# Linear attention and routed experts: the transposed q in two banks of its own, a tail step earlier, another front order

## The chip, the cores and the metric

The kernel runs on one core of a Trainium2 chip. Its engines work side by side, each through a queue of its own in order: PE multiplies matrices into PSUM, DVE and ACT do elementwise work and read PSUM, POOL does elementwise work in SBUF and issues loads, SP issues most other DMAs. The metric is the time of the program on the device in microseconds (us). The kernel before takes 950.27 us, the median of 3 runs from 950.16 to 950.39.

## What is computed

Inputs are q, k, v of shape (8, 8, 576, 64): 8 batches, 8 heads, 576 positions, 64 channels. Linear attention comes first, then a layer of 8 experts over 4608 tokens of 512 channels, weighted by a routing matrix that is normalised eight times over rows and columns.

```
phi(x) = where(x > 0, x, exp(x) - 1) + 1
q_p, k_p = phi(q), phi(k)
kv = einsum('bhsd,bhse->bhde', k_p, v);  z = sum(k_p, axis=2)
x  = (q_p @ kv) / (q_p . z + 1e-06)          # regrouped to (4608, 512)
P  = exp(x @ w_gate - max)
8 times: P /= P.sum(1) + 1e-09; P /= P.sum(0) + 1e-09; P *= 4608 / 8
out = sum over e of P[:, e] * (relu(x @ w1[e]) @ w2[e])
```

w1 is (8, 512, 1024), w2 is (8, 1024, 512).

## The kernel before

The program has three parts: a front, in which the attention is computed and expert 0 fills the gaps; a long middle, in which experts 1 to 7 run; and a tail for the last group of tokens.

**Attention by half batches.** The function att(b, g) handles four heads of a batch, half batch n = 2b + g, n from 0 to 15. Loads of k, q and v come through POOL's queue (n = 0 partly through SP's). Each kind has three buffers, so a load waits until the work on the load three before it is done. From k, ACT makes Exp and DVE makes max(x + 1, 1) and then the minimum of both, which is phi(k). PE multiplies it with v (f_kv, 64 x 64 tiles of the array). For q, PE transposes first (f_qt), into PSUM; ACT takes Exp of the transposed q (f_qe, L537), DVE the max (f_qm, L541), and DVE the minimum of both in SBUF (L550). Then PE forms denominators in two chunks (f_den), ACT takes Ln of them and Exp of the negative as reciprocal (f_ln, f_ex), PE forms numerators (f_num), and DVE multiplies into xT (f_x, L592), the transposed input of the experts.

**Banks.** The transposed q lies in the tile at2, two banks of PSUM, one for each pair of heads in fp16. The same two banks take the denominators, and for one allocation each the logits (L609). For half batch 1 alone the transposed q lies in the banks ye0 and ye1, and Exp and max each run on a half: ACT takes half 0 while DVE takes half 1, then they change. Otherwise ACT takes Exp of both banks in one instruction, and DVE max after it. For the last batch (n = 14, 15) the output of both is written in another order of positions. The banks ye0 and ye1 are otherwise where layer 2 of expert 0 accumulates (unit_plain, f_y, L1101): row tiles tt = 0, 2 in ye0 and tt = 1, 3 in ye1, emptied by ACT (L363) or DVE (L365).

**Expert 0** runs in groups g of 512 tokens: layer1 (L797: eight blocks of four 512-column matmuls into the two hq banks, emptied by L802 and L804), then layer 2 as four row tiles of two such blocks. Groups 0 to 3 run plainly within the front. Later groups, and all groups of experts 1 to 7, use a scheme with seven products in place of eight, in layer 1 (block7, pair, L912) and layer 2 (layer2, L1217, steps y1 to y7 with their evictions L1248, L1255, L1258). The blocks of xT and their sums are stored to DRAM through SP's queue (x_blocks) and loaded back for experts 1 to 7 (x_load). Small reads on SP (f_gs) hold those stores back until the loads of half batches 14 and 15 have landed.

**Routing** (sinkhorn) starts after the last logits: each of eight rounds goes POOL, DVE, POOL, DVE, PE (a column sum, L655), DVE.

**The order.** A planner (_Plan) holds a task for each piece of work, with its engines, an estimated cost, its dependencies and the buffer groups that it acquires or uses. Its first part is fixed by hand: _FRONT lists 2240 task numbers, each with the engine that takes it (p PE, a ACT, d DVE, g POOL, s SP, m a transfer, n nothing). The rest is placed by the planner's costs and priorities, with the order of PE's work in the middle and tail given by a chain.

**Tail.** The last group is not done with seven products: the function last gives it twelve steps z0 to z11 of plain matmuls, two for each of six pieces of output (z0, z1 for rows 384 to 511 of the group, z2, z3 for rows 256 to 383, and so on, the last ones narrow), in banks hq and R alternately, each piece with one eviction (L1322) and its output DMA. A string orders them among the steps y of the group before it.

Of the kernel before, what the change touches and what calls it, by code (L numbers as in the profile page):

```python
# [144 lines left out]
119g 120m 59a 28p 81n 82n 29p 85d 83a 30p 31p 86a 60p 77n 149g 150m 84d 78p 62a 87d 32p 79a 33p 61a  # L145
64p 34p 65d 35p 121g 122m 63a 36p 88p 66p 89a 37p 67d 38p 39p 92a 113g 114m 90p 94p 607p 91a 95d 115g
116m 608p 93a 157p 96p 159n 158n 609p 160a 97d 610p 611p 161d 613p 612a 615p 162d 174g 175m 617p 619p 614d 172g 173m
152d 621p 620a 151a 623p 124d 201g 202m 129p 622d 123a 153d 199g 200m 130p 625p 132n 131n 125d 133a 154n 176g 177m 155p
643n 618a 134d 156a 98n 99p 626d 100p 126n 103g 104m 163p 127p 135d 164a 616d 128a 165p 170p 624d 166a 101p 102p 228g
229m 167a 136p 627p 137a 629p 171d 168p 138p 169d 203g 204m 628p 139a 140a 630p 635d 232g 233m 143p 637d 184p 631p 185n  # L150
186n 187a 144d 633p 179d 178a 188d 634p 180d 255g 256m 141p 641a 211p 142d 230g 231m 632p 212n 213n 214a 206d 257g 258m
644p 189d 646p 215d 181n 205a 645d 182p 207d 284g 285m 648p 183a 234a 647d 288g 289m 190p 235d 650p 191a 208n 216d 649a
192p 209p 193a 652p 210d 259g 260m 194a 651d 311g 312m 197p 217p 654p 218a 198d 653a 236d 195p 219p 662p 220a 196d 237n
655a 262d 240p 238p 242n 241n 639d 243a 656p 315g 316m 239d 261a 244d 658p 291d 221a 226p 338g 339m 676n 245d 286g 287m
659d 224p 227a 246p 225d 664p 247a 657d 290a 267p 263d 222p 268n 665p 269n 270a 223d 365g 366m 264n 663p 313g 314m 271d
265p 670a 272d 248p 677p 249a 266d 292d 250a 273p 253p 666p 274a 254d 667p 317a 672d 275p 318d 251p 679p 276a 293n 252d
296p 680a 678d 294p 298n 297n 299a 319d 681p 342g 343m 277a 394g 395m 300d 683p 340g 341m 301d 295a 660p 344a 682d 369g
370m 302p 280p 367g 368m 303a 685p 281d 684a 278p 686d 304p 320n 661p 305a 279d 345d 323p 321p 325n 324n 326a 421g 422m
687p 322d 396g 397m 306a 327d 689p 328d 688a 282p 674a 346d 691p 372d 283a 690a 562d 309p 709n 329p 710p 330a 310d 569d
350p 711a 307p 351n 450g 451m 692d 695p 353a 347n 352n 308d 398g 399m 712p 668a 354d 371a 348p 570d 563d 331p 452g 453m  # L160
349a 696p 564d 332a 355d 448g 449m 714p 333a 713d 373d 334p 356p 716p 335d 357a 400a 715d 336p 358p 374n 401d 693p 359a
337d 478g 479m 718p 360a 717d 377p 402d 375p 378n 379n 480g 481m 380a 703d 457s 720p 482g 483m 458s 427a 459s 381d 699p
376d 719a 406p 361p 407n 423g 424m 694p 409a 362d 487s 382d 363p 701a 722p 408n 403n 410d 721a 488s 364d 383p 700p 384a
411d 723a 489s 385p 404p 565s 566m 386a 724p 405d 425g 426m 387a 412p 413a 490g 428d 388p 571d 697p 389d 725d 414p 390p
391d 455d 707a 415a 416a 429d 751p 417p 418d 433p 435n 434n 436a 437d 698p 705a 750n 454a 752a 732p 430n 431p 572s 573m
432a 576d 567s 568m 485d 438d 392p 393a 574s 575m 484a 577d 753p 439p 583d 486d 584d 578d 579s 580m 440a 581s 582m 730p
441p 419p 420d 755p 754a 442a 443a 494p 495n 497a 491n 496n 456d 756d 444p 445d 757p 731p 498d 758a 738a 759p 585d 446p
447d 463p 464n 466a 465n 733p 740a 492p 493a 760a 499d 467d 590d 761p 468d 500p 501a 762a 586s 587m 588s 589m 763p 502p
503a 504a 591d 746d 592d 460n 461p 462d 765p 469p 470a 505p 747d 506d 726p 748d 507p 766a 764a 508d 593s 594m 471p 472a
473a 749d 728p 729p 736a 767d 476p 477d 727p 734a 597g 768d 474p 773p 598n 771p 475d 560n 561p 772a 774a 789d 796n 790d  # L170
791d 792s 793m 742d 743d 509p 510a 512d 513g 511n 797p 798a 744d 745d 595s 596m 794s 795m 777p 778a 801p 802a 811p 514d
812a 775p 803p 804a 817p 515p 799p 807p 815p 818a 769d 847d 770d 516d 517g 800a 808d 821p 848d 849d 781p 813p 814a 816a
518d 519g 850s 851m 822d 805p 809p 810a 806d 779p 823p 776a 824a 852s 853m 819p 782d 520d 820d 780d 825d 855p 869p 870a
783p 521p 522d 826d 827d 828d 523g 599g 600m 784a 854n 873p 875p 831p 871p 876a 601g 602m 874a 872a 524d 525g 832a 856a
857p 879p 877p 878d 829p 858a 905d 526d 880d 906d 830a 861p 862a 859p 860a 835p 863p 527p 528d 865p 907d 908s 909m 866d
864d 836a 881p 529g 530d 882a 837p 839p 531g 1020s 1021m 1022s 1023m 840d 867p 963d 532d 868a 883d 833p 834a 913p 927p 928a
841p 933p 603n 912n 842a 533p 931p 932a 914a 934a 929p 930a 604g 605m 838d 964d 534d 884d 885d 535g 536d 965d 966s 967m
1024s 1025m 1026s 1027m 1028s 1029m 968s 969m 1030s 1031m 910s 911m 1032s 1033m 1062s 1063m 537g 915p 887p 888a 916a 889p 937p 935p
919p 893p 920a 1012d 538d 890a 936d 894a 938d 539p 540d 541g 917p 918a 886d 923p 924d 939p 897p 925p 895p 921p 926a 940a
542d 543g 898d 544d 922d 971p 899p 891p 545p 941d 900d 896d 546d 547g 970n 1013d 548d 972a 975p 976a 973p 977p 978a 985p  # L180
986a 987p 942d 1014d 549g 550d 988a 974a 892a 947p 991p 981p 982d 945p 979p 980d 992a 993p 983p 943d 946a 984a 995p 551p
552d 553g 989p 951p 952a 994d 996d 1015d 990a 949p 1034p 1036p 554d 1064s 1065m 1066s 1067m 1035a 955p 948d 555g 1040p 944d 997p
556d 953p 956d 1037a 1041a 1042p 954d 1038p 1044p 1039a 957p 1045d 998a 557p 1046p 958a 558d 1048p 559d 999p 1049a 1043d 1047a 1011n
1000p 1068s 1069m 702a 1016d 1070s 1071m 1050p 1072s 1073m 1017d 1054p 1051a 1074s 1075m 1001p 1018d 671a 706d 1056p 1055a 1052p 903a 1158s
1159m 1058p 1007a 1076p 1160s 1161m 1059d 1053a 1078p 1002p 1077a 1079a 1060p 1082p 1162s 1163m 1084p 1083a 1080p 642a 1086p 1003p 1061a 1087d
1081a 1057d 1004p 1008a 638d 669a 1088p 1132d 1090p 1089a 1019d 1092p 1091a 737d 1005p 1093a 1009d 1096p 1133d 1098p 1097a 1134d 1094p 950a
1100p 1085d 636a 1104p 1101d 1106p 1095a 1006p 1135d 1105a 640d 1107a 1102p 1010d 1110p 1103a 673d 1112p 1111a 741d 1108p 785d 843a 1136p
1099d 1138p 1137a 1141p 1140d 1139d 1114p 1144a 1146p 1109a 1115d 1145g 1142a 1149p 1148d 1143g 1147d 1116p 1151d 1118p 1113d 1117a 1120p 1164s
1119a 1152p 1166s 1165m 1121a 1124p 1153d 1167m 1126p 1150d 1125a 1168s 1122p 962d 1170s 1128p 1154d 1169m 1123a 1282s 1174p 1129d 1284s 1176p
1175a 1171m 1172n 1127d 1155p 1177a 675a 1283m 1130p 1157d 1180p 739d 1131a 1286s 1182p 1285m 1156d 1181a 1178p 1202d 786a 1206p 1287m 1203d  # L190
1208p 1204d 1207a 1179a 1205d 1211p 1183d 1184p 1212a 1209d 1216p 1214a 1210d 1213g 1185d 1219p 1218d 1186p 1221d 1188p 1217d 1187a 1190p 1215g
1173g 1528n 1529g 1531g 1532m 1530m 1220d 1189a 1222p 1191a 1194p 1256d 1196p 1195a 1223d 1192p 704a 1257d 1198p 1228p 1193a 1224d 1230p 1199d
1229a 1225p 1231a 1200p 1226d 1234p 1227d 1236p 1197d 1235a 1232p 1237d 1260p 1258d 1262p 1261a 1259d 1233a 1265p 1263d 708a 1238p 1268a 1264d
1270p 1201a 788d 1269g 1239d 904a 1273p 735d 1272d 1240p 1271d 1242p 1241a 1536d 1244p 1288s 1243a 1276p 1537d 1290s 1289m 1245a 1274d 844a
1248p 1277d 1291m 1250p 1538d 1292s 1249a 1246p 1294s 1266a 1278d 1252p 1293m 1247a 1406s 1298p 1253d 1408s 1300p 1299a 1295m 1296n 1251d 1279p
1301a 1254p 1281d 1304p 1275d 1410s 1255a 1306p 1280d 846a 1302p 1326d 1330p 1305a 1327d 1332p 1328d 1331a 1335p 1334d 1267g 1333d 1308p 1329d
1336a 1340p 1303a 787d 1337g 1309d 1343p 1342d 1310p 1345d 1312p 1341d 1311a 1314p 1297g 1533n 1534g 1535m 1344d 1313a 1346p 1307d 1315a 1318p
# [42 lines left out]
def kernel(  # L240
# [19 lines left out]
    NJ = S // PW  # L260
# [7 lines left out]
    S_ = _Plan()  # L268
    add = S_.add
# [19 lines left out]
    NR = B - 1  # L289
# [100 lines left out]
    def att(b, g):  # L390
# [1042 lines left out]
```

## Time and profile before

| what | us |
|---|---|
| time, median of 3 runs | 950.27 |
| the profiled execution's own time | 950.56 |
| its span, first to last instruction | 948.8 |
| PE busy | 938.9 |
| DVE busy | 766.0 |
| ACT busy | 574.7 |
| POOL busy | 157.3 |

The granted clock of TensorE is 0.999 over the span. Busy time is the time in which an instruction of the engine was under way; matmuls overlap and their ends are modelled, so a wait on PE can also hide in the distance between two starts. In the views that follow, columns are: for stretches, the stretch, its length, busy time and number of instructions of PE, weight loads, DVE, ACT, POOL, then granted clock, DMA share and GB/s; for groups, line, engine, operation, tiles and shapes with the count, then busy us, mean ns of one, and idle time before them with what ended it; for timelines and the chain of waits, start and length in us.

### The profile page before, as it was taken

What the parts mean: (1) busy time and instruction counts of PE and PEld (TensorE: products, weight loads), DVE (VectorE), ACT (ScalarE), POOL (GpSimd) and SP (SyncE); (2) the same over time, 40 slices, a digit from 0 to 9 for tenths busy, and PEclk for the clock granted to TensorE, in tenths of its full rate; (3) what the DMA queues carried; (4) which work ended last, traced back from release to release, by engine and by line L of the source; (5) the groups of instructions that cost most, each with busy time, mean ns of one, the idle gap of its engine ahead of it and who ended that gap; (6) DMA issues with size and microseconds to landing.
All of it is one profiled execution on the core that took longest, in us unless ns stands there. A gap on an engine that the chain in (4) does not pass through costs nothing.

```text
span 948.8 us, 20003 instructions
## 1 busy us (share of the span) xinstructions
PE 938.9 (99%) x7863; PEld 637.0 (67%) x7863; DVE 766.0 (81%) x1469; ACT 574.7 (61%) x1023; POOL 157.3 (17%) x222
## 2 busy tenths in 40 slices
PE   9999999999999999999999999999999999999997
PEld 4454488666676666766677666766667666776665
DVE  6889999778877888888887888778887888777776
ACT  6889866766655555555555555555555555555552
POOL 5432033011111111211011111111112111111110
PEclk9999999999999999999999999999999999999999
DMA  9999567244355222652236222652226422215554
GB/s 242 265 216 207 155 165 170 78 114 115 95 130 98 67 70 78 161 123 79 78 90 117 78 78 79 155 115 69 71 68 141 108 79 79 73 45 167 167 134 134
DMA packets 82570, 112.75 MB, mean 119 GB/s; under 512 B 7340, under 2 KB 46764, under 8 KB 82476
## 3 DMA queue, kind: packets, MB, share of 16 engines
q1 hardware_dynamic: 56876, 75.59, 26.3%
q0 software_dynamic: 24848, 34.78, 19.8%
q8 instruction: 61, 1.00, 0.4%
q10 hardware_dynamic: 752, 1.11, 0.3%
q14 instruction: 33, 0.27, 0.1%
HBM read 119.69 MB, written 17.69 MB: 145 GB/s over the span
## 4 chain that ended last, share of the span: by engine, by line
PE 90%; DVE 5%; DMA 3%; POOL 1%; issue 1%; ACT 0%; DVEq 0%; POOLq 0%
PE ye L1217 35%; PE hq L912 23%; PE R L912 12%; PE Zye L1217 6%; PE Zye L912 6%; PE ye L1101 3%; DMA w<-in_moe_w_dram 3%; PE hq L797 2%; DMA vv<-in_v_dram 1%; DVE hb L946 1%; DVE xT L1188 1%; PE kv_ps L454 1%; PE att L558 0%; PE att L484 0%; PE hq L1313 0%
## 5 line engine op out<-in xcount | busy, mean ns | idle before, releaser
L1248 DVE SCALAR_TENSOR_TENSOR acc<-ye,P_sb,acc 128x256 f32<-128x256 f32 x620 | 268.2, 479 | 126.7 <-PE ye L1217 124.3
L1217 PEld LDWEIGHTS <-S 128*128 128x128 f16 x1984 | 194.0, 98 | 46.6 <-DVE S L1188 0.2
L1258 POOL TENSOR_TENSOR acc<-acc,st 128x256 f32<-128x256 f32 x124 | 88.1, 730 | 632.2 <-ACT st L1255 627.7
L1217 PE MATMUL ye<-T,S 128*128 128x256 f16 x1488 | 192.8, 273 | 0.0
L1217 PEld LDWEIGHTS <-hb 128*128 128x128 f16 x1584 | 155.0, 98 | 42.9 <-issue 1.1
L912 PEld LDWEIGHTS <-W 128*128 128x128 f16 x1248 | 122.1, 98 | 86.5 <-issue 0.2
L943 ACT ACTIVATE hb<-hq 128x512 f16<-128x512 f32 x134 | 79.9, 597 | 140.8 <-PE hq L912 134.4
L912 PE MATMUL hq<-xs,W 128*128 128x512 f16 (+1 forms) x560 | 150.0, 358 | 0.0
L912 PE MATMUL R<-xs,W 128*128 128x512 f16 (+1 forms) x560 | 150.0, 358 | 0.0
L912 PE MATMUL hq<-xs,w 128*128 128x512 f16 (+1 forms) x560 | 139.8, 358 | 0.0
L912 PEld LDWEIGHTS <-w 128*128 128x128 f16 x936 | 91.6, 98 | 59.3 <-issue 0.6
L940 ACT ACTIVATE hb<-Zye 128x512 f16<-128x512 f32 x134 | 80.0, 597 | 40.9 <-PE Zye L912 40.3
L946 DVE CUSTOM_DVE_ANT_0 hb<-hq,sx 128x512 f16<-128x512 f32 x126 | 86.5, 686 | 20.0 <-PE hq L912 18.6
L1255 ACT ACTIVATE st<-Zye,P_sb 128x256 f32<-128x256 f32 x124 | 52.4, 471 | 76.2 <-PE Zye L1217 76.0
L933 ACT COPY sx<-hq 128x512 f32<-128x512 f32 x126 | 73.4, 583 | 37.2 <-PE hq L912 37.2
L946 DVE CUSTOM_DVE_ANT_0 hb<-R,sx 128x512 f16<-128x512 f32 x126 | 86.3, 685 | 4.7 <-ACT sx L933 3.6
L929 ACT COPY Zye<-hq 128x512 f32<-128x512 f32 x134 | 77.8, 581 | 19.7 <-PE hq L912 19.5
L1188 DVE TENSOR_TENSOR S<-hb 128x1024 f16<-128x1024 f16 x124 | 84.8, 684 | 4.6 <-ACT hb L943 4.6
L912 PE MATMUL Zye<-xs,w 128*128 128x512 f16 (+1 forms) x280 | 75.0, 358 | 0.0
L937 ACT COPY sx<-R 128x512 f32<-128x512 f32 x126 | 74.5, 591 | 0.4 <-PE R L912 0.4
L1217 PE MATMUL ye<-w,hb 128*128 128x256 f16 x528 | 68.4, 273 | 0.5 <-DVE acc L1248 0.5
L1217 PE MATMUL Zye<-w,hb 128*128 128x256 f16 x528 | 68.4, 273 | 0.0
(129 smaller groups left out, 946.4 us busy)
## 6 DMA issues: line engine op xcount, KB each, us to landing
xs<-xd SPq DMA_DIRECT2D x196, 256.0 KB, 3.5
w<-in_moe_w_dram POOLq DMA_DIRECT2D x17, 512.0 KB, 7.4
kin<-in_k_dram POOLq DMA_DIRECT2D x15, 576.0 KB, 7.9
out_dram<-acc SPq DMA_DIRECT2D x61, 128.0 KB, 2.4
w<-in_moe_w_dram POOLq DMA_DIRECT2D x7, 1024.0 KB, 9.6
xs<-xd SPq DMA_DIRECT2D x49, 128.0 KB, 3.4
vv<-in_v_dram POOLq DMA_DIRECT2D x16, 288.0 KB, 7.5
hb<-in_q_dram POOLq DMA_DIRECT2D x15, 288.0 KB, 8.0
```

The source lines that it names most:

```text
L912: nc.tensor.matmul(dst_[:, p, :] if parts == 2 else dst_.rearrange("p a b -> p (a b)"), lhsT=lhs(p, c), rhs=blk[i](c), start=(first and p ...
L929: nc.scalar.copy(out=Zt[1], in_=gX["tile"])
L933: nc.scalar.copy(out=gs2["tile"], in_=gX["tile"])
L937: nc.scalar.copy(out=gs5["tile"], in_=gR["tile"])
L940: nc.scalar.activation(out=dst(0, 0), in_=Zt[1], func=AF.Relu)
L943: nc.scalar.activation(out=dst(1, 0), in_=gX["tile"], func=AF.Relu)
L946: nc.vector._custom_dve(TENSOR_ADD_SAT, out=out_, in0=ps, in1=sb, s0=3.0e38, s1=0.0)
L1188: nc.vector.tensor_tensor(out=Sx[:, i], in0=a0, in1=a1, op=op)
L1217: nc.tensor.matmul(bank(g_)[:, s, :], lhsT=lhs(s, kk), rhs=rhs(kk), start=(new and s == 0 and kk == 0), stop=(kk == 3), skip_group_check=True)
L1248: nc.vector.scalar_tensor_tensor(out=dst(), in0=bank(g_)[:, s, :], scalar=P_sb[:, gg, e:e + 1], in1=dst(), op0=ALU.mult, op1=ALU.add)
L1255: nc.scalar.mul(out=gst["tile"], in_=bank(g_)[:, s, :], mul=P_sb[:, gg, e:e + 1])
L1258: nc.gpsimd.tensor_tensor(out=dst(), in0=dst(), in1=gst["tile"], op=ALU.add)
```

## The change

Five edits are made together.

1. Half batches 4 to 15 get what only half batch 1 had: the transposed q in ye0 and ye1, Exp and max on a half each, in four instructions instead of two. Half batches 0, 2 and 3 keep at2.
2. For the last batch, the other order of positions is written a half at a time.
3. In the order of the tail, z2 moves from behind y3 to the very front.
4. Four estimates of the planner change: the latency of late loads, the costs of Exp and max in halves, and one POOL step of the routing.
5. _FRONT is replaced by another list of 2268 entries. It holds the 24 new tasks and four more of the later ones. The loads, the products, evictions (some on the other engine) and stores stand in another order from the loads of half batches 6 and 7 and from layer 2 of the first group on; the start is the same. Task numbers above half batch 4 shift by two for each half batch.

```diff
-1n 606n 105n 112n 40s 41m 42s 43m 2p 3p 0g 4p 44g 45m 5p 6p 68g 69m 7p 8p 70g 71m 9p 72g
+1n 630n 105n 112n 40s 41m 42s 43m 2p 3p 0g 4p 44g 45m 5p 6p 68g 69m 7p 8p 70g 71m 9p 72g
...
-            tin[nm] = fadd(("dma", 1.425), lambda _: None, deps=[ti], use=[gr, *gsw], prio=pr, lat=1.95 if n < 2 else 2.4,
+            tin[nm] = fadd(("dma", 1.425), lambda _: None, deps=[ti], use=[gr, *gsw], prio=pr, lat=1.95 if n < 2 else 2.4 if n < 12 else 2.9,
...
-        ga = [S_.grp(p_ye[0]), S_.grp(p_ye[1])] if n == 1 else [S_.grp(p_att), S_.grp(p_att)]
+        own = n not in (0, 2, 3)
+        ga = [S_.grp(p_ye[0]), S_.grp(p_ye[1])] if own else [S_.grp(p_att), S_.grp(p_att)]
...
         def qin(hh):
-            if n == 1:
+            if own:
                 return ga[hh]["tile"].bitcast(FP16)[:, 0:S].rearrange("p (j w) -> p j w", w=PW)
             return qps()[:, hh]
 
         def f_qt(_):
-            for hh in range(2 if n == 1 else 0):
+            for hh in range(2 if own else 0):
                 ga[hh]["tile"] = yps.tile([P, 512], FP32, tag=f"ye{hh}", name=f"ye{hh}")
...
-            if n == 1:
+            if own:
+                if b >= NR:
+                    return dst[:, hs].rearrange("p (w j) -> p w j", j=NJ), qin(hs).rearrange("p j w -> p w j")
                 return dst[:, hs], qin(hs).rearrange("p j w -> p (j w)")
-            if b >= NR:
-                return dst.rearrange("p h (w j) -> p h w j", j=NJ), qps().rearrange("p h j w -> p h w j")
             return dst, at2.bitcast(FP16)[:, :, 0:S]
...
-            for hs in range(2 if n == 1 else 1):
+            for hs in range(2 if own else 1):
...
-                    c = (0.46 if dve else 0.6) if n == 1 else (0.76 if b < NR else 1.36) if dve else 1.13
+                    c = ((0.46 if b < NR else 0.7) if dve else 0.65) if own else 0.76 if dve else 1.13
                     pair.append(fadd(("dve", c) if dve else ("act", c), f_qm if dve else f_qe,
-                                     deps=[ta if dve else t0, *pair], use=[*([ga[hs]] if n == 1 else ga), gq if dve else geq], prio=pr))
+                                     deps=[ta if dve else t0, *pair], use=[*([ga[hs]] if own else ga), gq if dve else geq], prio=pr))
...
-                last = [add(("pool", 0.9), f_a, deps=last, prio=-200.0)]
+                last = [add(("pool", 0.95), f_a, deps=last, prio=-200.0, lat=0.1)]
...
-              for x in "y1 y5 z0 y2 y6 z1 y3 z2 z3 y7 z4 z5 y4 z6 z7 z8 z9 z10 z11".split()]
+              for x in "z2 y1 y5 z0 y2 y6 z1 y3 z3 y7 z4 z5 y4 z6 z7 z8 z9 z10 z11".split()]
```

More of the change, by code (lines that the diff above doesn't have):

```diff
@@ L146 @@
[L146 to L160, printed above, removed]
@@ L232 @@
[L232 to L235 removed]
+119g 120m 59a 28p 81n 82n 29p 85d 83a 30p 31p 86a 60p 77n 149g 150m 84d 78p 62a 87d 32p 33p 79a 61a
@@ new lines @@
+64p 34p 65d 121g 122m 35p 63a 36p 88p 66p 89a 37p 67d 38p 39p 113g 114m 92a 90p 94p 631p 91a 95d 115g
+116m 632p 93a 157p 96p 159n 158n 633p 160a 97d 634p 635p 161d 637p 636a 639p 174g 175m 162d 641p 643p 638d 172g 173m
+152d 645p 644a 151a 647p 124d 203g 204m 646d 129p 123a 153d 201g 202m 130p 649p 125d 132n 131n 133a 154n 176g 177m 155p
+667n 642a 134d 156a 98n 99p 650d 100p 126n 103g 104m 163p 127p 135d 164a 640d 128a 165p 170p 648d 166a 101p 102p 232g
+233m 167a 136p 651p 137a 653p 171d 168p 138p 205g 206m 169d 654p 139a 140a 652p 661d 141p 659a 657p 142d 143p 178a 658p
@@ new lines @@
+144d 179d 668p 665a 180d 261g 262m 184p 669a 670p 234g 235m 186n 185n 189d 187a 208d 190a 265g 266m 672p 188d 671a 191d
+207a 181n 182p 673d 213p 236g 237m 674p 215n 214n 183d 216a 218d 292g 293m 238a 209d 192p 676p 263g 264m 239d 193a 210n
+217d 211p 350g 351m 219a 675d 194p 655p 294g 295m 195a 212d 220d 267a 656p 240d 678p 196a 677d 199p 679d 221p 663a 680p
+222a 200d 244p 223p 197p 245n 323g 324m 247a 682p 246n 241n 198d 224a 296g 297m 249d 242p 700n 683a 248d 681d 230p 243a
+250a 268d 684p 251d 231a 321g 322m 225a 269d 252p 226p 685p 253a 299d 298a 227d 690p 692d 228p 254p 229d 270n 691p 255a
@@ new lines @@
+256a 701p 698d 300d 273p 271p 274n 275n 352g 353m 276a 278d 703p 272d 279a 410g 411m 277d 702a 280d 259p 325g 326m 304p
+705p 260d 305n 307a 354g 355m 704a 328d 381g 382m 257p 281p 306n 301n 707p 258d 282a 308d 327a 283p 309d 302p 708d 688p
+310a 357d 303a 356a 689p 329d 311d 686p 696a 379g 380m 358d 284a 687p 439g 440m 706a 383g 384m 285a 286p 312p 586d 709p
+313a 287d 711p 694a 710d 314p 288p 333p 315a 289d 330n 713p 335n 334n 412g 413m 336a 338d 712d 339a 331p 337d 316a 715p
+414g 415m 332d 340d 714a 362p 733n 716d 317p 341p 363n 441g 442m 365a 734p 318d 342a 587d 319p 385a 736p 320d 364n 359n
@@ new lines @@
+367d 735a 343p 360p 366d 368a 386d 361a 472g 473m 369d 721p 722p 344a 345a 737d 348p 729d 600d 349d 370p 371a 416a 417d
+719p 720p 346p 347d 387d 372p 738p 727a 468g 469m 500g 501m 477s 391p 388n 392n 393n 396d 373a 374a 418d 377p 378d 470g
+471m 740p 739a 394a 290p 395d 375p 601d 376d 397a 291a 742p 422p 423n 502g 503m 424n 389p 445a 741a 744p 588d 398d 425a
+390a 399p 419n 420p 478s 427d 428a 446d 426d 602d 429d 745d 507d 723p 400a 421a 404p 401p 479s 509s 506a 504g 505m 402a
+403a 717p 718p 743d 508d 510s 511s 443g 444m 405d 725a 474a 724p 731d 746p 406p 430p 431a 447d 407d 451p 453n 452n 448n
@@ new lines @@
+456d 512g 454a 455d 748p 774n 457a 747a 432p 433a 449p 749d 754p 755p 458d 450d 475d 435p 476d 589s 590m 434a 762a 459p
+460a 436d 603s 604m 775p 776a 516p 517n 461p 462a 593d 594d 437p 438d 519a 518n 513n 595d 521d 520d 607d 591s 592m 596s
+597m 598s 599m 777p 778a 463a 408p 514p 522a 523d 515a 779p 780a 409a 483p 464p 484n 465d 608d 609d 610s 611m 605s 606m
+781p 524p 486a 466p 467d 480n 485n 488d 525a 782a 783p 784a 481p 526p 489a 487d 527a 614d 785p 482a 490d 750p 615d 616d
+529p 617s 618m 528a 530d 770d 612s 613m 491p 492a 787p 788a 619s 620m 771d 493p 494a 495a 531p 532d 756p 757p 764a 786a
@@ new lines @@
+498p 751p 772d 499d 496p 789p 790a 752p 773d 497d 584n 813d 814d 533p 534a 535n 871d 753p 758a 815d 766d 816s 817m 1044s
+1045m 536d 537g 767d 768d 585p 821p 822a 820n 538d 795p 825p 835p 796a 799p 621g 769d 627n 622n 791d 826a 836a 539p 540d
+872d 760a 800d 873d 792d 793d 818s 819m 823p 824a 827p 828a 841p 842a 623g 624m 541g 542d 874s 875m 829p 797p 543g 830d
+845p 839p 801p 794d 831p 802a 837p 832d 838a 798a 544d 846d 840a 805p 806d 843p 844d 833p 834a 1046s 1047m 1048s 1049m 545p
+546d 547g 847p 848a 849d 803p 879p 893p 895p 894a 628g 629m 896a 929d 548d 549g 850d 804d 550d 807p 899p 897p 808a 853p
@@ new lines @@
+900a 878n 898a 880a 851d 903p 904d 551p 552d 553g 854a 625g 626m 901p 885p 886a 859p 883p 860a 884a 930d 902d 905p 881p
+882a 889p 906a 554d 555g 863p 855p 856a 931d 852d 887p 932s 933m 556d 890d 557p 558d 891p 892a 559g 857p 987d 937p 951p
+952a 864d 865p 866a 1050s 1051m 1052s 1053m 1054s 1055m 1056s 1057m 858a 560d 957p 861p 958a 561g 888d 911p 562d 563p 907d 908d
+909d 912a 936n 953p 564d 954a 955p 961p 862d 565g 956a 917p 962d 566d 1036d 567g 938a 939p 943p 988d 944a 963p 959p 989d
+568d 990s 991m 964a 913p 941p 947p 940a 945p 948d 960d 915p 914a 942a 918a 910d 946d 949p 921p 569p 916a 570d 571g 1086s
@@ new lines @@
+2187a 2184d 2191p 2189d 2190d 2164p 2192a 2185d 2196p 2194a 2193g 2165d 2700m 2199p 2195g 2197d 2198d 2166p 2200d 2168p 2201d 2167a 2170p 2169a
+2202p 2220s 2171a 2221m 2174p 2203d 2176p 2204d 2175a 2172p 2250d 2330s 2178p 2173a 2331m 2177d 2222p 2332s 2224p 2179d 2223a 2333m 2205p 2251d
+2225a 2180p 2252d 2228p 2206d 2181a 2334s 2230p 2207d 2229a 2335m 2226p 2253d 2254p 2227a 2231d 2256p 2255a 2259p 2257d 2258d 2232p 2260a 2264p
+2262a 2233d 2261g 2267p 2263g 2265d 2266d 2234p 2268d 2236p 2269d 2235a
```

128 lines of the change are left out of this document (52 added, 76 removed).

## The prediction

> **What bounds the kernel now.** I read the page's engine rows first, then busy time by stage, then who waited for whom, then the chain of waits around the longest wait. The engine rows name the bound: PE.
>
> ```profile
> PE 938.9 (99%) x7863; PEld 637.0 (67%) x7863; DVE 766.0 (81%) x1469; ACT 574.7 (61%) x1023; POOL 157.3 (17%) x222
> ```
>
> Busy time by stretch (first number: length; then PE, PEld, DVE, ACT, POOL) shows where PE still has something to give:
>
> ```profile
> 0.00:30.00 30.00, 27.54 (x415) 12.50 (x416) 20.85 (x33) 20.61 (x28) 16.70 (x27) 1.00 1.11 235
> 30.00:120.00 90.00, 88.36 (x1498) 43.39 (x1496) 81.37 (x134) 77.35 (x105) 22.90 (x33) 1.00 0.88 208
> 120.00:170.00 50.00, 49.44 (x454) 43.75 (x452) 47.71 (x105) 30.35 (x56) 15.18 (x18) 1.00 0.66 158
> 170.00:260.00 90.00, 89.92 (x603) 58.63 (x601) 74.00 (x144) 62.81 (x117) 11.68 (x17) 1.00 0.41 106
> 260.00:920.00 660.00, 660.00 (x4724) 462.12 (x4723) 524.52 (x1021) 376.67 (x707) 88.00 (x123) 1.00 0.38 100
> 920.00:949.00 29.00, 23.68 (x180) 16.66 (x178) 17.57 (x35) 6.92 (x14) 2.83 (x4) 0.97 0.46 127
> ```
>
> From 260 to 920 us PE has no idle time, and the change does not touch that stretch. In the first 30 us the order of PE's work is the same in both fronts. So the open accounts are the idle time from 30 to 260 us, 1.64 + 0.56 + 0.08 = 2.28 us, and the tail. The answer on waits names the two longest pieces of the idle time after the start:
>
> ```profile
> PE kv_ps L454 <- DMA vv<-in_v_dram: 1.1, 1, 1.1
> PE ye L1217 <- DVE acc L1248: 0.5, 1, 0.5
> ```
>
> Half of the 2.28 us is one wait for a v load. The second row is in the tail. The whole visible saving is then a few us of 950: this is a change of some tenths of a per cent either way, and a measurement of this kernel tells about 0.2% (1.9 us) from nothing.
>
> **The change, part by part.** PE's arithmetic is the same before and after. Only waits and the switches between 64-row work (transposes, k-v products, denominators, numerators) and 128-row work can move its end.
>
> *Switches.* The chain of waits (start, length) around the longest wait shows their price:
>
> ```profile
> 88.56 0.25 PE att L558 x4
> 88.81 0.53 PE kv_ps L454 x36
> 89.34 0.29 issue
> 89.63 6.72 DMA vv<-in_v_dram
> 96.35 0.14 issue
> 96.49 0.70 PE kv_ps L454 x36
> ...
> 100.27 0.25 PE att L558 x4
> 100.52 0.12 PE num_ps L558 x4
> 100.64 0.97 PE hq L797 x4
> ...
> 103.11 0.86 PE ye L1101 x4
> 103.98 0.86 PE hq L797 x4
> ```
>
> Four 512-column matmuls take 0.86 us before other 128-row work and 0.97 before 64-row work, so a switch costs about 0.1 us. I take 0.09. I counted the switches in the two front orders: 107 before, 103 after. Four fewer: -0.37 us.
>
> *The v load of half batch 13.* It is the last load in POOL's queue in both orders, and with three v buffers it waits for the k-v product of half batch 12 (88.81). From there to the product of 13 the load needs 0.53 + 0.29 + 6.72 + 0.14 = 7.68 us. PE's work put between the two is this, from the next row on, where the matmuls before the wait run 93.46 + 1.83 = 95.29:
>
> ```profile
> 93.46 1.90 PE L1101 MATMUL ye<-w,hb 128*128 128x512 f16 x8
> ```
>
> That is 95.29 - 88.81 = 6.48 us, hence a wait of 1.2. (8 matmuls at 0.216 and a switch make the 1.83.) The new order has six blocks of four 512-column matmuls between the two products where there were five, as many small groups, and six switches instead of eight: 6.48 + 0.87 - 0.18 = 7.17. The wait falls to 0.5 us: -0.7. Bounds: if the load is faster because the stores of xT no longer start beside it, all 1.2 go; if it is 0.7 slower, none.
>
> *Halves in own banks.* For half batches 4 to 15 Exp and max run on halves, as half batch 1 does already. The chain of waits near the front's end has the whole form of the last batch, from transpose to denominators:
>
> ```profile
> 105.09 0.39 PE att L484 x36
> 105.48 0.02 issue
> 105.50 1.14 ACT eq L537
> 106.64 0.02 issue
> 106.67 1.37 DVE qpT L541
> 108.03 0.04 issue
> 108.08 0.32 PE att L558 x4
> ```
>
> All forms (count, busy, mean ns):
>
> ```profile
> L537 ACT ACTIVATE eq<-att 128x1152 f16<-128x1152 f16 x14 | 15.8, 1126 | 3.1 <-PE att L484 2.8
> L541 DVE TENSOR_SCALAR qpT<-att 128x1152 f16<-128x1152 f16 x14 | 11.8, 840 | 1.5 <-ACT eq L537 1.3
> L537 ACT ACTIVATE eq<-ye 128x576 f16<-128x576 f16 x2 | 1.2, 647 | 0.0
> L541 DVE TENSOR_SCALAR qpT<-ye 128x576 f16<-128x576 f16 x2 | 0.9, 458 | 0.3 <-ACT eq L537 0.3
> L365 DVE COPY qpT<-att 128x1152 f16<-128x1152 f16 x1 | 0.8, 758 | 0.0
> L363 ACT COPY acc<-ye 128x512 f32<-128x512 f32 x21 | 12.2, 586 | 3.9 <-PE ye L1217 2.4 <-PE ye L1101 1.5
> L365 DVE COPY acc<-ye 128x512 f32<-128x512 f32 x7 | 4.7, 676 | 0.8 <-PE ye L1101 0.8
> L425 ACT ACTIVATE ek<-kin 128x1152 f16<-128x1152 f32 x16 | 18.5, 1162 | 2.7 <-DMA kin<-in_k_dram 2.7
> ```
>
> ACT: 2 x 0.647 - 1.126 = +0.168 us a half batch, +2.0 for twelve. DVE: 2 x 0.458 - 0.758 (a copy of that size; 0.840 is a mean with the two slow strided ones of the last batch) = +0.16 for ten, +1.6. For the two of the last batch, whose strided form takes 1.37 us whole (106.67), halves of 0.458 would be -0.45 each and a strided half is not shown; I take 0, the stride being the same, with +0.16 as the other end. By the new order three evictions net move from DVE to ACT (0.676 against 0.586), so DVE ends near -0.4 and ACT near +3.8 us over the front. ACT idles 90 - 77.35 = 12.65 us from 30 to 120. I cost the added work at zero because this idle time covers it; where the cover fails, it costs up to 3.8 us.
>
> [...]
>
> What it buys: one bank pair less in contention. In the last half batches Exp and max of the transposed q sit in the chain, and the denominators that want the same banks wait behind them (105.09 to 108.08 above).
>
> Serial that is 1.14 + 1.37 = 2.5 us. With two banks ACT takes one half while DVE takes the other, about 2 x 0.65 = 1.3 us, and the denominators' banks stay free. [...]
>
> What it costs: the banks are those into which layer 2 of expert 0 accumulates (ye0, ye1). A transpose now waits until both were evicted, 0.59 us on ACT or 0.68 on DVE (rows above), with some 0.05 on either side (108.03 to 108.08). In the new order the last layer-2 block ends one block of 0.87 and a switch, 1.0 us, ahead of the transposes of half batches 4 and 7, 1.2 ahead of 13, 1.4 ahead of 11 and 15: 0.2 to 0.7 us of slack at five places. Behind the transpose in PE's queue stands everything else. If the evicting engine has just begun an Exp of 1.16 us (the row of ek), a place costs up to 1.16 - 0.2, about 1.0. Bounds for all the small waits from 30 to 260 us, now 2.28 - 1.1 = 1.2: all vanish (-1.2), or the five places cost 0.5 each on top of half of the old (+1.9). I take -0.3, near the rows' present level, since the orders are equally dense.
>
> *Logits and routing.* The attention's last numerator has three blocks of 0.87 us and four switches fewer ahead of it, 3.0 us, but the last column sum of the routing has about as much PE work ahead as before. Steps in SP's and POOL's queues move (stores of groups 0, 2, 1; the last three raw stores behind ten loads of blocks; the loads for 7 and 10 earlier; expert 1's weights among the first routing steps). Each keeps a load's length of several us in hand, and I cost them at zero; a late one costs at most its overhang, as the v load shows. Costs that only the planner sees change nothing inside the fixed list.
>
> *Tail.* The four matmuls of step z2 (the first half of the sum for output rows 256 to 383 of the last group) move ahead of y1. In the timeline:
>
> ```profile
> 929.78 0.59 PE L912 MATMUL hq<-xs,w 128*128 128x512 f16 x2
> 929.91 0.88 DVE L1248 SCALAR_TENSOR_TENSOR acc<-ye,P_sb,acc 128x256 f32<-128x256 f32 x2 [0.18 <-PE ye L1217]
> 930.85 0.38 PE L1217 MATMUL ye<-w,hb 128*128 128x256 f16 x2 [0.47 <-DVE acc L1248]
> ...
> 932.67 1.03 PE L1313 MATMUL hq<-w,hb 128*128 128x512 f16 x4
> ```
>
> PE is free at 929.78 + 2 x 0.216 = 930.21 and y1 starts at 930.85, when DVE has emptied its bank: 0.64 us. z2 needs h of the first half, long there, and a free bank of R. It fills 0.87 us, so y1 starts at 931.08, 0.23 late, and 0.87 is gone later: -0.64. The gap it leaves, z1 y3 z3 between y6 and y7, still has 2.6 us, against 0.2 + 2 x 0.44 us of DVE that y7 waits for. Its eviction and output DMA hang on z3 and stay behind it. Bound: 0 if the DVE falls behind, -0.64 in full.
>
> Sum: -0.37 - 0.7 - 0.3 - 0.64 = -2.0 us, all on the path, since PE is the path. The profiled execution had a span of 948.8 and a time of 950.56, 0.3 over the median of 950.27. So 948.6 for a profiled one, and 948.3 for the median.
>
> **The rivals.** (1) *New waits replace the old.* The five ye places and the denser ACT give the v load's gain back: -0.37 - 0.64 + 0.2 = -0.8, so 949.5. For it: ACT 77 of 90 us and DVE 81 of 90 busy, little room. Against: the shorter 1.3 us chain. (2) *All waits of the front go*, and the v load lands in time: -0.37 - 0.64 - 2.28 = -3.3, so 947.0. Against: the counted 7.17 us. (3) *Slower.* ACT is the front's bound in disguise: its +3.8 us, in a front that is to be 3 us shorter, would leave 12.65 - 3.8 - 3 = 5.9 us idle of 87. If dependencies do not let it use that, q's Exp runs late, ye0 and ye1 are held, and layer 2 of expert 0 stops behind them in PE's queue: up to 3.8 - 1.0 = +2.8, so 953.1. It decides from the point where the front's own waits grow by more than 1.0 us. (4) *Half of it does nothing*: z2's bank or data not free, tail unchanged: 948.9.
>
> **How the numbers follow.** Chances: forecast, 948.3, from 947.6 to 948.9: 0.42; (4) 0.05; (1) 0.28; (2) 0.17; (3) 0.08. The range leaves out the lower half of (2) and (3) but its edge, 0.15 together: 946.9 to 950.1. Faster by over 0.2% needs 948.37 or less: some 0.25 of the forecast's 0.42 and all of (2), 0.42. Slower by over 0.2%, 952.17 or more, is the larger part of (3): 0.05. Within: 0.53.
>
> **What would show it.** In the profile after: PE's wait of k-v product for the v load at about 0.5 instead of 1.1; no wait of y1 for the DVE in the tail, and z2 ahead of it; 26 half Exps of 0.65; idle time of PE from 30 to 260 us near 1.3. Wrong it would be where new rows of transposes (L484) waiting for ACT or DVE, or of ye (L1101) waiting for eq or qpT, sum to more than 1 us.

## The result, and the profile after

The changed kernel takes 947.93 us (median of 16 runs, 947.29 to 948.79), the kernel before 949.94 beside it on the same chip (16 runs, 948.97 to 951.27). The ratio is 0.9976, with a 95% interval of 0.9969 to 0.9983: faster by about 2 us. The forecast was 948.3, and its sum of terms -2.0 us.

The profiled execution took 947.83 us with a span of 946.1, against 950.56 and 948.8: 2.7 us between these two. All code lines have moved down by one or two (L454 is now L455, L484 is L486, L1217 is L1219). From the page of the kernel after, the engine rows:

```profile
PE 938.4 (99%) x7863; PEld 637.5 (67%) x7863; DVE 764.8 (81%) x1478; ACT 575.5 (61%) x1038; POOL 157.5 (17%) x222
```

The kernel after, busy time by stretch, with the columns of the prediction's table:

```profile
0.00:30.00 30.00, 28.00 (x414) 12.67 (x415) 20.62 (x33) 20.49 (x28) 16.67 (x27) 1.00 1.10 234
30.00:120.00 90.00, 89.39 (x1513) 45.08 (x1512) 83.94 (x153) 79.73 (x122) 25.01 (x35) 1.00 0.94 223
120.00:170.00 50.00, 49.68 (x457) 44.19 (x456) 45.13 (x99) 30.55 (x57) 13.28 (x16) 1.00 0.58 132
170.00:260.00 90.00, 89.92 (x597) 58.08 (x596) 74.96 (x144) 62.42 (x117) 11.69 (x17) 1.00 0.41 106
```

PE's idle time from 30 to 260 us is 0.61 + 0.32 + 0.08 = 1.01 us, where it was 2.28. ACT and DVE are fuller from 30 to 120 us (79.73 and 83.94 us, from 77.35 and 81.37), partly since more of the front's work now fits into the stretch: PE is too. The kernel after, who waited for whom on PE (us in total, times, longest):

```profile
PE yw L693 <- DVE hb L683: 1.3, 1, 1.3
PE att L560 <- ACT rden L572: 0.3, 1, 0.3
PE ye L1103 <- DMA w<-in_moe_w_dram: 0.2, 1, 0.2
PE kv_ps L455 <- DVE xT L594: 0.2, 1, 0.2
```

The first row is at the start, the same before and after. The wait for the v load and the wait of y1 in the tail are gone, and no new row of transposes (L486), or of ye for eq or qpT, has come: what the prediction named as the mark of the slower rivals is absent. The v load of half batch 13 reads so in the timeline of the kernel after (start, length; the first row is the k-v product of 12, the last that of 13):

```profile
85.66 0.67 PE L455 MATMUL kv_ps<-vv,t 64*64 64x128 f16 x36
...
86.65 0.71 POOL L412 DMA_DIRECT2D vv<-in_v_dram  x1 [0.75 <-PE kv_ps L455]
...
91.08 0.84 SPq L862 DMA_DIRECT2D xd<-acc  x2
...
92.96 0.67 PE L455 MATMUL kv_ps<-vv,t 64*64 64x128 f16 x36
```

The view of tile vv, same kernel, from 80 to 100 us, gives the time from issue to landing of the two loads there:

```profile
DMA to landing us min/median/max: 5.6/5.7/5.9
```

The load of 13 is the 5.9: it lands at 86.65 + 5.9 = 92.55, and the product's turn comes at 92.96, 7.30 us after that of 12. There is 0.4 us in hand. The stores of xT (91.08) now start 4.4 us after the load's issue. In the kernel before, where the load is issued at 89.63, they started 0.34 us after it. Its timeline has the product of 12 and those stores so:

```profile
88.64 0.67 PE L454 MATMUL kv_ps<-vv,t 64*64 64x128 f16 x36
...
89.97 1.23 SPq L860 DMA_DIRECT2D xd<-acc  x2
```

The timeline of the tail of the kernel after:

```profile
927.77 0.59 PE L914 MATMUL hq<-xs,w 128*128 128x512 f16 x2
927.90 0.88 DVE L1250 SCALAR_TENSOR_TENSOR acc<-ye,P_sb,acc 128x256 f32<-128x256 f32 x2 [0.18 <-PE ye L1219]
...
928.20 1.02 PE L1315 MATMUL R<-w,hb 128*128 128x512 f16 x4
...
929.06 1.04 PE L1219 MATMUL ye<-w,hb 128*128 128x256 f16 x8
```

z2 (L1315, into R) fills the gap, and y1 starts behind it with no wait. From the first of these matmuls to the end of the span it was 948.8 - 929.78 = 19.02 us, and is 946.1 - 927.77 = 18.33: -0.69. That same matmul starts 929.78 - 927.77 = 2.01 us earlier, which is the front's share. Of it, 0.46 us is idle time before 30 us (28.00 us busy against 27.54), where both kernels have the same order of work: that much belongs to the two executions, not to the change (over all profiles of this document PE's busy time there runs from 26.6 to 28.1 us). So the change itself shows about -2.3 us here, and -2.0 between the medians.

### The profile page after: what moved, and what is told of

Read it like the earlier page. It is cut to its first block, busy times and chain, and to the rows that moved or that the text cites. A ratio compares the mean times of both kernels' runs of the same rounds, so it can differ in the third digit from the quotient of the medians.

```text
span 946.1 us, 20024 instructions
## 1 busy us (share of the span) xinstructions
PE 938.4 (99%) x7863; PEld 637.5 (67%) x7863; DVE 764.8 (81%) x1478; ACT 575.5 (61%) x1038; POOL 157.5 (17%) x222
## 4 chain that ended last, share of the span: by engine, by line
PE 91%; DVE 5%; DMA 3%; issue 1%; POOL 1%; ACT 0%; DVEq 0%; POOLq 0%
PE ye L1219 36%; PE hq L914 24%; PE R L914 12%; PE Zye L914 6%; PE Zye L1219 6%; PE ye L1103 3%; DMA w<-in_moe_w_dram 3%; PE hq L799 2%; DVE xT L594 1%; PE kv_ps L455 0%; PE num_ps L560 0%; PE hq L1315 0%; DVE xT L1190 0%; DVE hb L948 0%; DVE qpT L543 0%
## 5 line engine op out<-in xcount | busy, mean ns | idle before, releaser
L1219 PEld LDWEIGHTS <-S 128*128 128x128 f16 x1984 | 194.0, 98 | 46.5
L1219 PE MATMUL ye<-T,S 128*128 128x256 f16 x1488 | 192.8, 273 | 0.0
L1219 PEld LDWEIGHTS <-hb 128*128 128x128 f16 x1584 | 155.0, 98 | 42.6 <-issue 0.7
L1219 PE MATMUL ye<-w,hb 128*128 128x256 f16 x528 | 68.4, 273 | 0.1
L1219 PE MATMUL Zye<-w,hb 128*128 128x256 f16 x528 | 68.4, 273 | 0.0
```

The source lines that it names most:

```text
L1219: nc.tensor.matmul(bank(g_)[:, s, :], lhsT=lhs(s, kk), rhs=rhs(kk), start=(new and s == 0 and kk == 0), stop=(kk == 3), skip_group_check=True)
```

## The experiments

### Each half alone: the tail step, and the front

```diff
-"y1 y5 z0 y2 y6 z1 y3 z2 z3 y7 z4 ..."
+"z2 y1 y5 z0 y2 y6 z1 y3 z3 y7 z4 ..."
```

This is the kernel before with the tail's new order (tail_only). The other (front_only) is the kernel after with the old string.

> The kernel before with the tail's new order alone (z2 ahead of y1). My theory: the wait of y1 for the DVE, 0.64 us, is filled and nothing else changes: 0.6 us faster than before (0.9993). Rival (z2 not ready, or the DVE falls behind): no change. Other rival (the whole gain of 2 us is the tail): 2 us faster.

> The changed kernel with the old order of the tail. My theory: the front alone gives 1.4 to 2.0 us (0.9985 to 0.9979), with the tail's wait of 0.5 to 0.6 us back. If the front gave nothing, the time would be that of before.

> The changed kernel again, beside the parts on the same chip. If front and tail add up, its gain over before is that of both parts together, about 2.0 us (0.9979); if they share a wait, it is less than their sum.

Measured on one chip, the kernel before at 950.39: the tail alone 949.38, ratio 0.9985 [0.9976, 0.9993]; the front alone 948.43, ratio 0.998 [0.997, 0.9989]; both 947.93, ratio 0.9972 [0.996, 0.9983]. (A ratio here is not exactly that of the two medians.) Both parts gain: 1.0 and 2.0 us by the medians, against 2.5 for both together, which agrees within the intervals. The tail's share by time is loose, 1.0 us here (interval 0.7 to 2.3) and 0.5 between front_only and the whole. Its size is read from the timelines. The tail's gain is the wait of y1: the timeline of tail_only has z2 and y1 back to back,

```profile
930.27 1.02 PE L1313 MATMUL R<-w,hb 128*128 128x512 f16 x4
931.13 1.04 PE L1217 MATMUL ye<-w,hb 128*128 128x256 f16 x8
```

and that of front_only has the old wait of 0.47 us again:

```profile
928.60 1.03 PE L1219 MATMUL ye<-w,hb 128*128 128x256 f16 x8 [0.47 <-DVE acc L1250]
```

The profile of tail_only held something not expected. Its front is that of the kernel before, yet the v load is not waited for: the product of half batch 13 starts at 95.20 with no wait for it. The stores started 2.1 us after the load's issue (0.34 in the profile of before). The lost time comes back elsewhere in the timeline of tail_only: DVE waits 1.07 us for a store, and PE 1.05 us for the xT that stands behind it in DVE's queue:

```profile
89.54 0.97 POOL L411 DMA_DIRECT2D vv<-in_v_dram  x1 [3.63 <-PE kv_ps L454]
...
91.61 0.84 SPq L860 DMA_DIRECT2D xd<-acc  x2
...
95.20 0.70 PE L454 MATMUL kv_ps<-vv,t 64*64 64x128 f16 x36
...
98.98 0.43 DVE L842 TENSOR_TENSOR acc<-xT 128x512 f16<-128x512 f16 x1 [1.07 <-DMA xd<-acc]
...
101.80 0.32 PE L558 MATMUL num_ps<-qpT,kvz 64*64 64x288 f16 x4 [1.05 <-DVE xT L592]
```

So the wait that the prediction priced is not there in every execution of the old order. It need not come back elsewhere either. The profile of added_work (below), which has the old order too, shows neither loss: its last v load, from issue to landing, takes 4.4 us (4.3 in tail_only, 6.7 in the profile of before), and the product has no wait for it. Its timeline:

```profile
89.61 0.97 POOL L411 DMA_DIRECT2D vv<-in_v_dram  x1 [3.62 <-PE kv_ps L454]
...
91.38 0.83 SPq L865 DMA_DIRECT2D xd<-acc  x2
...
95.27 0.70 PE L454 MATMUL kv_ps<-vv,t 64*64 64x128 f16 x36
```

In all three profiles the stores start 0.34 us after the landing of the v load ahead of this one (89.63 in before, 91.27 in tail_only, 91.04 in added_work), so it is that landing which differs between executions. PE's idle time from 30 to 260 us is 2.28, 2.36 and 1.42 us in these three profiles with the old order (before, tail_only, added_work), and 1.01, 0.97 and 1.27 in three with the new one (after, front_only, whole): 2.0 against 1.1 in the mean.

### The v load taken out by a fourth buffer

```diff
-    NV, NK, NQ = 3, 3, 3
+    NV, NK, NQ = 4, 3, 3
```

Once in the kernel before (four_v), once in the kernel after (after_four_v).

> The kernel before with four v buffers in place of three, so that the v load of half batch 13 waits for the k-v product of 11 and not of 12. The order is as before. My theory: PE's wait of 1.1 us for that load is gone and the program is about 1.1 us faster (0.9988). Rival: the wait is hidden by slack behind it, or another wait takes its place: faster by less than 0.4 us.

> The changed kernel with four v buffers, so that the last v load no longer waits for the k-v product of half batch 12. Theory: the new order has no wait left for this load, so it is within 0.4 us of the changed kernel. If the load were still late in many executions, it would be 0.5 us or more faster than the changed kernel's 947.9 and the best so far.

Before: 949.63 against 950.39, ratio 0.9991 [0.9982, 1.0]. After: 947.77 against 950.33 for the kernel before, ratio 0.9973 [0.9963, 0.9983], which is 0.16 us from the 947.93 without it, no difference. In four_v the wait is gone from the list, and the stretch of busy time shows it:

```profile
30.00:120.00 90.00, 89.63 (x1509) 44.55 (x1508) 82.50 (x138) 78.15 (x106) 22.59 (x33) 1.00 0.90 212
```

PE is 1.27 us fuller there than in the kernel before. By the medians a fourth buffer is worth some 0.8 us in the old order, but the interval reaches from 1.7 us to none: the time alone does not decide between the 1.1 us expected and the rival's 0.4 or less. In the new order it is worth nothing, and no profile of that order has a row for this wait: the new order has itself taken it away.

### The halves without banks of their own

In halves_shared the kernel before gets Exp and max on halves, and nothing else: q stays in at2, the new instructions stand beside the old ones in the list. In halves_late the second half stands where DVE's old max stood.

```diff
+        cut = n not in (0, 2, 3)
...
-            for hs in range(2 if n == 1 else 1):
+            for hs in range(2 if cut else 1):
```

> The kernel before, with Exp and max of half batches 4 to 15 cut in halves but still in the two shared banks, and the 24 new instructions put in beside the old ones; the order is otherwise that of before. It adds the work (ACT about 2.0 us, DVE about 1.6) and takes some serial time off each half batch. My theory: the added work is hidden and PE's order does not use the shorter chain: within 0.5 us of before. Rival (ACT and DVE are the bound of the front): 1.5 us or more slower.

> The halves in the shared banks in the order of before, as in the run before (halves_shared, 6.8 us slower), but the two instructions of the second half stand in the order where DVE's old max stood, not where ACT's old Exp stood. So ACT is not held behind DVE early. Theory (hand-overs in queues that are in order): the cost depends on the place, and here it is clearly other than 6.8 us, 2 to 5 us. Rival (the cost is the work of the halves itself): 6 to 7.5 us again.

Both are slower by far more than was expected: 956.87 against 950.07, ratio 1.0072 [1.0059, 1.0085], and 959.15 against 950.33, ratio 1.0093 [1.0079, 1.0106]. The place does matter, by some 2 us, but the later place is the worse one, not the better. Groups by form, halves_shared (busy and mean ns, then idle time before them and what ended it):

```profile
L539 ACT ACTIVATE eq<-att 128x576 f16<-128x576 f16 x24 | 15.6, 648 | 9.2 <-DVE qpT L543 6.9 <-PE att L486 2.3
L543 DVE TENSOR_SCALAR qpT<-att 128x576 f16<-128x576 f16 x24 | 12.1, 506 | 7.6 <-ACT eq L539 7.3
```

The same groups of the kernel after:

```profile
L539 ACT ACTIVATE eq<-ye 128x576 f16<-128x576 f16 x26 | 16.4, 651 | 1.3 <-PE ye L486 1.1 <-DVE qpT L543 0.2
L543 DVE TENSOR_SCALAR qpT<-ye 128x576 f16<-128x576 f16 x26 | 12.5, 495 | 0.5 <-ACT eq L539 0.4
```

The instructions cost the same, 0.65 us a half on ACT. The idle time ahead of them does not: 9.2 and 7.6 us, against 1.3 and 0.5. The timeline of halves_shared says why, here for one half batch:

```profile
62.79 0.65 ACT L539 ACTIVATE eq<-att 128x576 f16<-128x576 f16 x1
...
63.47 0.46 DVE L543 TENSOR_SCALAR qpT<-att 128x576 f16<-128x576 f16 x1 [0.41 <-ACT eq L539]
...
63.96 0.65 ACT L539 ACTIVATE eq<-att 128x576 f16<-128x576 f16 x1 [0.52 <-DVE qpT L543]
...
64.64 0.46 DVE L543 TENSOR_SCALAR qpT<-att 128x576 f16<-128x576 f16 x1
```

The four take turns, each starting 0.03 us after the one ahead of it has ended, and in all twelve half batches they stand in turns, at this distance or a longer one. The likely reason is that at2 is one tile for the program, whichever half of it is read; the trace itself shows only the turns. In the timeline of the kernel after, with two tiles, both engines work at once:

```profile
92.29 1.25 ACT L539 ACTIVATE eq<-ye 128x576 f16<-128x576 f16 x2
92.41 1.01 DVE L543 TENSOR_SCALAR qpT<-ye 128x576 f16<-128x576 f16 x2
```

So cutting in halves is a loss by itself, of 6.8 to 9 us: the pair needs three hand-overs in place of one, and whatever stands behind the waiting half in either queue waits too (0.52 us on ACT and 0.41 on DVE in the half batch above). The halves of at2 also lie in two banks; what the kernel after has and this one lacks is two tiles. An at2 made of two tiles, with the transposed q where it was, was not run, so whether two tiles alone would do is open.

### The banks without the order, and the order without the banks

own_old_order is the kernel after with the front order and the tail of the kernel before; shared_new_order is the kernel after with q back in at2. In both, a piece of work that cannot stand where the list has it, because its bank is still held, is put off to the first place where it can. First a line of the list as it changes in own_old_order, then the edit of shared_new_order:

```diff
-64p 34p 65d 121g 122m 35p 63a 36p 88p 66p 89a 37p 67d 38p 39p 113g 114m 92a 90p 94p 631p 91a 95d 115g
+64p 34p 65d 35p 121g 122m 63a 36p 88p 66p 89a 37p 67d 38p 39p 92a 113g 114m 90p 94p 631p 91a 95d 115g
```

```diff
-        ga = [S_.grp(p_ye[0]), S_.grp(p_ye[1])] if own else [S_.grp(p_att), S_.grp(p_att)]
+        ga = [S_.grp(p_ye[0]), S_.grp(p_ye[1])] if n == 1 else [S_.grp(p_att), S_.grp(p_att)]
```

> The code of the changed kernel (own banks, halves) with the front order of before, in which only those tasks are put off that the banks ye0 and ye1 make impossible where they stood (28 places on PE), and the old tail. My theory: the banks bring nothing without an order made for them; transposes and layer 2 of expert 0 wait for each other and it is 0 to 3 us slower than before. Rival: the banks are the gain: at least 1 us faster than before.

> The changed kernel with the new order and the halves, but with the transposed q of half batches 4 to 15 back in the two shared banks; only the tasks that this makes impossible are put off (18 places on PE, 13 on ACT). My theory: the new order leans on the banks; denominators and transposes wait for one another and it is 1 to 3 us slower than the changed kernel, so near before. Rival: the order is the gain and the banks do not matter: within 0.4 us of the changed kernel (947.9, 2.0 to 2.5 below before).

own_old_order took 998.61 us against 950.07, ratio 1.0497 [1.0479, 1.0515], and shared_new_order 978.09, ratio 1.0298 [1.0277, 1.0318]. Both expectations were too small by tens of us. The banks without an order for them cost 48 us, the order without the banks 28. The stretch from 30 to 120 us in own_old_order,

```profile
30.00:120.00 90.00, 67.02 (x913) 31.54 (x912) 51.18 (x86) 48.48 (x68) 20.58 (x28) 0.81 0.68 148
```

and in shared_new_order:

```profile
30.00:120.00 90.00, 76.65 (x1200) 35.63 (x1201) 64.78 (x112) 65.81 (x93) 22.64 (x32) 0.92 0.79 177
```

PE does 913 matmuls there, and 1200, of the 1513 of the kernel after. The longest rows of who waited for whom, own_old_order:

```profile
PE att L560 <- DVE qpT L552: 9.1, 5, 2.6
PE num_ps L560 <- DVE xT L594: 6.5, 4, 2.6
PE att L560 <- ACT rden L572: 5.9, 7, 1.4
```

Transposes put off until ye0 and ye1 are free make q late, and then denominators, numerators and xT are waited for with nothing left to do between them. The put-off also rearranges the order, so these two runs don't price the banks alone; they show that code and order were fitted to each other, and that the prediction's five places with 0.2 to 0.7 us in hand hold by the list, not by the code.

### The price of a switch

Ten pieces of attention work in the kernel after are moved behind the next block of 128-row work, which makes twenty more switches (124 for 104 in its front). One of the ten:

```diff
-... 675d 194p 655p 294g ...
+... 675d 655p 194p 294g ...
```

> The changed kernel with ten denominators or numerators put one block of matmuls later in PE's order, so that 20 switches between 64-row and 128-row work are added (124 for 104). My theory: 0.093 us each, 1.9 us slower than the changed kernel, so about the time of before. Rival (a switch is hidden by weight loads or waits): less than 0.6 us slower.

952.21 us, ratio 1.0019 [1.0006, 1.0031] to the kernel before, so 4.3 over the median of the kernel after, where 1.9 was expected. From the distances between starts in its trace, a 512-column matmul before 64-row work takes 309 ns (median), before 128-row work 216: 93 ns a switch, 1.86 us for twenty. (The traces of before and after have the same two medians.) That price does not explain the other 2.4 us. About 1.1 us of them is idle time of PE (span less busy time is 950.3 - 941.5 = 8.8 us, against 946.1 - 938.4 = 7.7), 1.0 of it in this stretch (89.39 us busy before the move), as where ten products come late for what follows. The rest lies within PE's busy time and was not traced. The stretch in this run:

```profile
30.00:120.00 90.00, 88.42 (x1476) 41.51 (x1475) 80.36 (x143) 77.00 (x116) 22.59 (x32) 1.00 0.89 212
```

The price of 0.09 stands by the starts; the time of this run alone would not have separated it from the waits.

### The added work alone

In the kernel before, each Exp and each max of half batches 4 to 15 is followed by a small copy that nothing waits for.

```diff
+                    if n >= 4:
+                        nc.scalar.copy(out=extra[:, 0, 0:8], in_=ones_t[:, 0:8])
...
+                    if n >= 4:
+                        nc.vector.tensor_copy(out=extra[:, 1], in_=ones_t[:, 8:72])
```

> The kernel before with one small copy of a constant put behind each Exp on ACT (about 0.2 us, twelve) and each max on DVE (about 0.1 to 0.15 us, twelve) of half batches 4 to 15. Nothing waits for them: it is the added work of the halves without their hand-overs. Theory: the 6.8 us of the halves in the old order came from ACT and DVE waiting for each other in the middle of a half batch, and added work alone costs less than 1.0 us. Rival: ACT and DVE are the bound of the front, and 3.5 us of work costs 2.5 us or more.

950.34 against 950.33, ratio 1.0002 [0.9993, 1.0011]. Groups by form, added_work:

```profile
L545 DVE COPY extra<-ones_t 128x64 f32<-128x64 f32 x12 | 2.6, 217 | 0.0
L539 ACT COPY extra<-ones_t 128x8 f32<-128x8 f32 x12 | 2.3, 191 | 0.0
```

2.3 us more on ACT and 2.6 on DVE, 0.19 and 0.22 us a copy (0.1 to 0.15 was expected on DVE), and PE pays nothing. Both engines have room for the added time; what they have no room for is to wait for each other (halves_shared adds about as much work and costs 6.8 us).

## Why the prediction was right

The forecast was 948.3 with a sum of -2.0 us; measured were -2.0 between the medians and a ratio whose interval, put on the 950.27 shown, gives 947.3 to 948.7. It held the forecast, and left out rival (2) at 947.0 and rivals (1), (3) and (4). Term by term, in the two traces:

| term | predicted | shown by the two traces |
|---|---|---|
| switches | -0.37 | four fewer at 0.093: -0.37 |
| v load of half batch 13 | -0.7 | -1.1 in these two, no wait left |
| small waits, 30 to 260 us | -0.3 | 2.28 - 1.1 to 1.01: -0.2 |
| tail | -0.64 | -0.69 |
| halves, added work | 0 | 0 (added_work) |
| sum | -2.0 | -2.3, and -2.0 by the medians |

The agreement to a tenth is in part luck, since executions of one kernel differ by as much as a term: with the means over three profiles, idle time from 30 to 260 us falls by 0.9 (2.0 to 1.1) where the prediction had 0.7 + 0.3 = 1.0, and the sum is -2.0. The time of the front alone shows that the front gains; how its gain divides between the load and the switches rests on the traces.

**Switches.** Right in count and price, by the starts. (The trace of the kernel after has 104 up to 120 us, and that of before 108; the prediction's lists gave 103 and 107.)

**The v load.** The mis-sized term. The prediction counted from the chain of waits, which starts the product of 12 at 88.81; the timeline has 88.64, so 0.17 goes on both of its sums. Then the work between the two products was well counted, 7.17 + 0.17 = 7.34 us predicted and 7.30 shown. The load's side was taken over unchanged, 7.68 + 0.17 = 7.85 us, and was 86.65 - 85.66 = 0.99, the transfer's 5.90, and the same 0.14 behind it: 7.03. All of the 0.82 between them is the transfer, 5.90 against 6.72. The bound "all 1.2 go" named the case, and it is the one that came in this profile. Its reason, that the stores of xT no longer start beside the load, is not shown, and it fits the rows only in part. With the stores 0.34 us after the issue the load took 6.72, with 2.1 and 1.8 us (tail_only, added_work) 4.3 and 4.4. But in the kernel after the stores come latest of all, 4.4 us after the issue, and the load takes 5.90. There the v load ahead of it is issued only 1.5 us earlier (85.18) and lands at 90.74, so the two share most of their time; whether that is the cause was not tried. No run held the stores back by themselves, since DVE's sums wait for them. The term also treated as fixed what differs between executions of the kernel before: in the profile of tail_only the same order had no wait there, and paid 1.05 us for xT instead, and in that of added_work it paid neither.

**Small waits.** -0.2 for -0.3. The five places where transposes follow an eviction closely gave no row in the answer on PE's waits, neither the +1.9 of the upper bound nor rival (1).

**Halves.** Zero was right, and the reason given, ACT's idle time, is borne out by added_work. The halves are 0.651 us as taken from half batch 1, 26 of them. For the strided halves of the last batch DVE takes 1.41 us the pair in the timeline of the kernel after, against 1.37 whole, so the 0 taken there was right too:

```profile
103.86 1.41 DVE L543 TENSOR_SCALAR qpT<-ye 128x576 f16<-128x576 f16 x2
```

What the step left unsaid is its condition. It priced 24 more instructions by their length, and the experiments show that the length is the harmless part: the same halves in one tile cost 6.8 us, and in two tiles in the wrong order 48.

The gain was sought in a shorter chain, 1.3 for 2.5 us, and that is not what came. The 2.5 is of the last batch alone. From the start of the first to the end of the last of a half batch's Exp and max, half batches 4 to 15 take 1.90 to 2.58 us in the kernel before, 2.00 in the median. In the kernel after they take 1.25 (the pair at 92.29) to 3.80, 2.46 in the median: the new order often puts other work between the halves. In the last of them the first Exp starts at 101.61, the DVE halves at 103.86 and the second Exp, beside the second DVE half, at 104.64: 3.7 us. Nothing is lost by it, since nothing of PE's waits there. The forecast put no gain on the shorter chain, so its sum did not suffer; but the argument "the shorter 1.3 us chain" against rival (1) did not hold, and what the banks of their own bring by themselves no run isolates.

That ACT and DVE work side by side on two banks is what the traces show. Half batch 1 in the timeline of the kernel before:

```profile
11.64 0.46 DVE L541 TENSOR_SCALAR qpT<-ye 128x576 f16<-128x576 f16 x1
11.74 1.18 ACT L537 ACTIVATE eq<-ye 128x576 f16<-128x576 f16 x2
12.42 0.46 DVE L541 TENSOR_SCALAR qpT<-ye 128x576 f16<-128x576 f16 x1 [0.32 <-ACT eq L537]
```

In the kernel after it is 1.25 and 1.01 us side by side, at 92.29 and 92.41. The banks do not explain the strict turns in at2, since its halves lie in two banks as well.

**Tail.** Right in mechanism, and in size by the timeline; the old string brings the wait back (0.47 us in front_only).

**Rivals.** (1), new waits in place of the old, and (3), ACT as the bound, have no row. Rival (2) had the v load right in this profile, but 1.01 us of other idle time stays. (4) fell with the tail.

## What to carry to other kernels

Where one engine is 99% busy, write down the few waits and switches left on it, price each from its row, and the sum can be right to some tenths of a us. Look at more than one profile before pricing a wait for a transfer: the longest wait priced here stood in one of three profiles of the old order. When an edit is said to shorten a chain, read the whole chain again in the profile after. When an elementwise step is cut in parts for two engines, price the hand-overs and ask whether the parts lie in separate tiles: here 2.3 us on ACT and 2.6 on DVE were free (added_work), while the halves that took turns cost 6.8 (halves_shared). A part of a change that is made together with its order can't be judged alone: without the other, each was a loss of 3 to 5%.

## What the runs showed of the hardware

In the two runs in which PE waited longest, its clock was lower as well. The granted clock was 1.00 from 30 to 120 us at 83.53 us of busy PE (halves_shared), 0.92 at 76.65 (shared_new_order) and 0.81 at 67.02 (own_old_order). It does not follow the busy time slice by slice: in own_old_order it was 0.67 from 70 to 80 us, with PE busy for 5.91 us, and 0.71 from 100 to 110 at 8.92, but 0.99 from 120 to 130 at 7.20. In the timeline of own_old_order:

```profile
72.02 3.43 PE L799 MATMUL hq<-xT,w 128*128 128x512 f16 x8
```

Eight such matmuls take 1.90 us in the prediction's row at 93.46, where the granted clock was 1.00 (93 to 96 us); here 3.43. So in these two runs the order cost twice, by the waits and by the clock, which is part of why 48 and 28 us were far from expected. The longest single wait in the list of own_old_order is 2.6 us, and its three longest rows are 16 waits, 21.5 us together. Whether it was the waits that brought the clock down, no run tried by itself.
